# Fold parts of a Fourier mixing kernel issued one step earlier, and the first batch's folds and mixes at other steps

## The chip, the cores and the metric

The kernel runs on one core of a Trainium2 chip. The metric is device time in microseconds (us). The engines are named as the profile names them: PE (TensorE matmuls), PEld (its weight loads), DVE (VectorE), ACT (ScalarE), POOL (GpSimd) and SP (SyncE, which here only issues DMAs). The kernel's data is float32 throughout.

## The reference

The input x has 8 batches of 3008 rows by 256 columns. Each batch is Fourier transformed along its rows and along its columns, and the real part is kept. The result, seen as 24064 rows, goes through a layer with 2048 hidden units.

```python
X = np.fft.fft(x, axis=1)
X = np.fft.fft(X, axis=2)
y = X.real.astype(np.float32).reshape(B * S, D)      # (24064, 256)
h = y @ w_in                                         # w_in (256, 2048)
g = h * (1.0 / (1.0 + np.exp(-1.702 * h)))
out = g @ w_out                                      # w_out (2048, 256)
```

## The kernel before

**Two kinds of work share the engines.** The transform of a batch comes first: its x is loaded into one large tile `xt` (`load_x`, L205), folded on POOL (`fold1`: sums and differences of mirrored columns and rows, in place), multiplied by cosines and sines on PE (`mix1`, L255), copied back into `xt` by ACT (`mixed`, L263), spilled to memory (`spill`, L339) and read back in another layout (`fill`, L345). A second stage on PE (`stage2`, L365) makes the operands `pq` of the hidden layer. The column transform is folded into `w_in`, which gives the weights `wcs`. While PE, ACT and DVE work through the hidden layer of batch b, the transform of batch b+1 is slipped in between.

**Steps.** The hidden layer runs in 384 steps t, 48 for each batch: 3 blocks, 2 halves of a block, and 8 steps p = t mod 8, each with two of the 16 groups of 128 hidden units. The first 8 steps of the program have a form of their own (`hidden`, `rows`). From t = 8 a step works as follows, each engine in this program order:

- PE makes the pre-activations: `begin(t, 1)` and `begin(t+1, 0)` (L184, into `x`). Bank `x` is filled beforehand by ACT with a rank-one term, two steps ahead: `middle(t+2)` (L585).
- ACT applies the activation to one half (`forward`, L600), doubles the sum (`doubled`, L597) and applies it to the other half (`activate_back`, L607), which DVE has made (`backward`, L604).
- The product with `w_out` uses a fast matrix multiplication of Strassen's kind, so that sums and differences of activations are needed: `sums(t, nc.gpsimd)` on POOL (L615, L616), `sums(t-1, nc.vector)` on DVE every second step (L622, L623), and a second level on DVE, `deeper` (L646 and L648 in odd steps, L650 in even ones).
- PE multiplies three steps later: `product(t-3)` (L184, into `o`) and `small_products` (L684, into `low` and `o`). At the first step after an output sum, the small products 5, 6 and 3 of the old group come right after `begin(t, 1)` (the flag `opening`, L1040).

**Output sums.** Every 8 steps an output is complete. It is put together in the steps p = 2 (`combine`, L754 to L758), 3 (`combine_small`, L786), 4 (`swap` L794 to L796 on ACT, `combine_last` L768 and L804) and 5 and 6 (`turn_last`, the transpose L737 on DVE, then stores on SP).

**Work of the transform.** A table `extra` lists calls to be made at the end of a step: `at(t, fn, ...)`. The folds of one batch are 16 calls: 8 chunks c, each with part 0 (L225, L227; for chunk 0 also three operations into the tile `e`, L218 to L220) and part 1 (L230, L231). Four calls, those of two chunks, make a group, and `mix1` of that group follows. POOL runs in order, so a fold part issued at the end of step t stands behind the sums of t and before the sums of t+1.

**What a mix changes in its step.** A step whose list holds `mix1` or `stage2` is called special (L1028). The mix takes the bank that x(t) has left, so `middle(t+2)` is not issued in that step but at the start of the next, and PE's order in the next step is another one (`after`, L1028: the products come ahead of `begin`).

**The table.** `PLANS` (L932) holds two plans, the first for b = 0 and the second for all later ones. Each has the 16 steps of the fold parts, the 4 steps of the groups, and the step of the first of three fills, counted from the first step of batch b. For later batches the folds of group m lay at 8m - 1, 8m, 8m + 1 and 8m + 2, which is p = 7, 0, 1, 2, and its mix at 8m + 7. Spills follow one step after a mix. `load_x` of batch b+2 is issued at steps 36, 38, 40 and 42 of batch b, `rotate` at 39, and `stage2` at 8, 24 and 40. In the first batch's steps 5 to 10 the last weights are made as well: differences on POOL (`differences`, L482) and on DVE (`small_weights`, L695).

Of the kernel before, what the change touches and what calls it, by code (L numbers as in the profile page):

```python
# [112 lines left out]
def kernel(ctx: ExitStack, tc, x, w_in, w_out, tab1, tab2, out):  # L113
# [815 lines left out]
    finish_out(0)  # L929

    extra, early = {}, {}
    PLANS = ((range(11, 27), (16, 20, 25, 28), 32), ([g + k for g in (0, 8, 16, 24) for k in range(-1, 3)], (7, 15, 23, 31), 33))  # L932

    def at(t, fn, *args):
        extra.setdefault(t, []).append((fn, args))
# [23 lines left out]
    for b in range(B):  # L959
# [5 lines left out]
        if b + 1 < B:  # L965
            folds, groups, filled = PLANS[min(b, 1)]
            for c in range(NCH):
                for part in range(2):
                    at(t0 + folds[2 * c + part], fold1, b + 1, c, part, nc.gpsimd)
                if c % 2:  # L970
                    k = t0 + groups[c // 2]
# [140 lines left out]
```

## Time and profile before

| | us |
|---|---|
| median of 3 runs | 1852.71 (1851.91 to 1855.34) |
| the profiled execution | 1851.27 |
| its span, first to last instruction | 1849.5 |
| PE busy | 1835.5 |
| DVE busy | 1485.5 |
| ACT busy | 1148.6 |
| POOL busy | 1001.1 |

Views used: the page; the list of waits (engine and line, what it waited for, us in total, times, longest); stretches (from:to, us, then busy us and count of PE, PEld, DVE, ACT and POOL, granted clock, share of the DMA queues' time, GB/s); and rows in order of time (start us, duration us, engine, line, operation, out<-in, count, and in brackets the idle time before it with what ended it). A row of the timeline may hold several equal instructions. A duration in the timeline counts from when the engine took the instruction up, so it contains any time in which the instruction was held up.

### The profile page before, as it was taken

The numbers are of one execution on the slowest core, as the hardware profiler recorded it, in microseconds if no ns is written. First come the engines' busy times: TensorE is split into PE (matmuls) and PEld (weight loads), VectorE is DVE, ScalarE is ACT, GpSimd is POOL, SyncE is SP. The second block draws the span as 40 slices with busy tenths as digits, with TensorE's granted clock in tenths as the row PEclk, the third lists the DMA queues.
The fourth block names the chain that finished last, engine by engine and source line by source line (L and its number), as shares of the span: only waits on it lengthen the run. The fifth ranks groups of instructions, "written<-read, shape, count | busy, mean of one in ns | idle before, by whom it ended". The sixth has DMA issues, their size and how long they took to land.

```text
span 1849.5 us, 55986 instructions
## 1 busy us (share of the span) xinstructions
PE 1835.5 (99%) x23722; PEld 1411.0 (76%) x23722; DVE 1485.5 (80%) x1928; ACT 1148.6 (62%) x2241; POOL 1001.1 (54%) x1053
## 2 busy tenths in 40 slices
PE   8999999999999999999999999999999999999998
PEld 5677777777777777777777777777788777778776
DVE  6988778887888778877788778878888788878875
ACT  5666656666666666666665666666655666656663
POOL 4786456554556546565365544656446654444442
PEclk9999999999999999999999999999999999999999
DMA  8721341214211151211502115121241112100111
GB/s 285 178 61 34 87 65 28 55 32 103 44 48 40 33 112 29 60 33 48 109 13 71 33 48 97 22 72 26 71 73 23 35 26 56 30 19 13 23 19 24
DMA packets 149706, 105.31 MB, mean 57 GB/s; under 512 B 106057, under 2 KB 130665, under 8 KB 148896
## 3 DMA queue, kind: packets, MB, share of 16 engines
q1 hardware_dynamic: 146624, 99.68, 24.0%
q8 instruction: 187, 3.06, 0.7%
q10 hardware_dynamic: 2832, 2.05, 0.5%
q14 instruction: 63, 0.52, 0.1%
HBM read 64.41 MB, written 48.05 MB: 61 GB/s over the span
## 4 chain that ended last, share of the span: by engine, by line
PE 88%; DVE 8%; DMA 2%; ACT 1%; issue 1%; POOL 0%; SPq 0%; DVEq 0%; ACTq 0%; POOLq 0%
PE x L184 32%; PE o L184 25%; PE low L684 23%; PE o L684 4%; PE ps L255 2%; DVE big L650 2%; PE ps L365 1%; DVE big L622 1%; DVE big L604 1%; DVE big L786 1%; DVE big L648 1%; DVE big L646 1%; DMA xt<-in_x_dram 1%; DMA Td<-big 1%; DVE big L804 0%
## 5 line engine op out<-in xcount | busy, mean ns | idle before, releaser
L615 POOL TENSOR_TENSOR big<-big 128x256 f32<-128x256 f32 (+1 forms) x376 | 357.9, 952 | 797.0 <-ACT big L607 694.5
L184 PE MATMUL x<-pq,wcs 128*64 128x256 f32 (+1 forms) x6016 | 776.8, 376 | 1.0 <-ACT x L585 0.4
L184 PE MATMUL o<-big,wo 128*64 128x256 f32 (+1 forms) x4800 | 629.0, 375 | 0.6 <-issue 0.6
L184 PEld LDWEIGHTS x<-pq,wcs 128*64 128x64 f32 x6016 | 421.9, 137 | 175.9 <-issue 15.3
L184 PEld LDWEIGHTS o<-big,wo 128*64 128x64 f32 x4800 | 348.0, 137 | 145.9 <-issue 1.0
L597 ACT ACTIVATE g<-x 128x512 f32<-128x512 f32 (+1 forms) x376 | 221.8, 590 | 379.9 <-PE x L184 378.6
L604 DVE TENSOR_TENSOR big<-g,x 128x512 f32<-128x512 f32 (+1 forms) x376 | 250.8, 667 | 186.5 <-ACT big L600 186.4
L616 POOL TENSOR_TENSOR big<-big 128x256 f32<-128x256 f32 (+1 forms) x376 | 399.6, 1063 | 0.0
L585 ACT ACTIVATE x<-nb,af 128x256 f32<-128x256 f32 (+1 forms) x752 | 353.0, 469 | 69.1 <-DVE pq L372 55.9
L684 PE MATMUL low<-big 128*64 128x128 f32 (+1 forms) x5888 | 386.1, 270 | 0.0
L684 PEld LDWEIGHTS low<-big 128*64 128x64 f32 x5888 | 341.0, 137 | 27.9
L600 ACT ACTIVATE big<-x 128x512 f32<-128x512 f32 (+1 forms) x376 | 219.2, 583 | 123.5 <-PE x L184 113.6
L646 DVE TENSOR_TENSOR big<-big 128x1024 f32<-128x1024 f32 (+1 forms) x184 | 234.1, 1272 | 65.2 <-PE low L684 41.4
L607 ACT ACTIVATE big<-big 128x512 f32<-128x512 f32 (+1 forms) x376 | 231.7, 616 | 37.2 <-DVE big L604 35.4
L684 PE MATMUL low<-big,wo 128*64 128x128 f32 (+1 forms) x2944 | 224.8, 271 | 1.4 <-DVE big L650 0.7
L648 DVE TENSOR_TENSOR big<-big 128x512 f32<-128x512 f32 (+1 forms) x184 | 177.1, 963 | 15.9
L650 DVE TENSOR_TENSOR big<-big 128x512 f32<-128x512 f32 (+1 forms) x184 | 185.4, 1007 | 0.0
L684 PEld LDWEIGHTS low<-big,wo 128*64 128x64 f32 x2944 | 175.4, 137 | 6.4 <-DVE big L650 2.9
L622 DVE TENSOR_TENSOR big<-big 128x512 f32<-128x512 f32 (+1 forms) x188 | 140.7, 748 | 3.3 <-POOL big L615 3.3
L623 DVE TENSOR_TENSOR big<-big 128x512 f32<-128x512 f32 (+1 forms) x188 | 135.6, 721 | 6.5
L684 PEld LDWEIGHTS o<-big,wo 128*64 128x64 f32 x1472 | 94.3, 137 | 24.3
L684 PE MATMUL o<-big,wo 128*64 128x128 f32 (+1 forms) x1472 | 112.2, 270 | 0.0
(97 smaller groups left out, 1144.6 us busy)
## 6 DMA issues: line engine op xcount, KB each, us to landing
out_dram<-os SPq DMA_DIRECT2D x284, 64.0 KB
t<-Td SPq DMA_DIRECT2D x22, 512.0 KB
Td<-xt SPq DMA_DIRECT2D x56, 192.0 KB
xt<-in_x_dram SPq DMA_DIRECT2D x14, 512.0 KB
xt<-Xr SPq DMA_DIRECT2D x14, 512.0 KB
nb<-Nd SPq DMA_DIRECT2D x23, 256.0 KB
out_dram<-os SPq DMA_DIRECT2D x96, 56.0 KB
Xr<-in_x_dram SPq DMA_DIRECT2D x7, 752.0 KB
```

The lines of the kernel that those rows point to most:

```text
L184: nc.tensor.matmul(out[c0:c0 + 64], lhsT=lhs[:, c0:c0 + 64], rhs=rhs, skip_group_check=True, **how)
L585: nc.scalar.activation(x[:, i * 256:i * 256 + n], nbt[b, blk][:, hh * 256:hh * 256 + n], ACTF.Copy, scale=af1[:, f:f + 1])
L597: nc.scalar.activation(two(g[:], n), two(xb[t][:], n), ACTF.Copy, scale=2.0)
L600: nc.scalar.activation(front(t), two(xb[t][:], width(t)), ACTF.Gelu_apprx_sigmoid)
L604: nc.vector.tensor_tensor(back(t), two(gt.pop(t)[:], n), two(xb.pop(t)[:], n), op=ALU.subtract)
L607: nc.scalar.activation(back(t), back(t), ACTF.Gelu_apprx_sigmoid)
L615: eng.tensor_tensor(right(t, S1, n), left(t, A21, n), right(t, A22, n), op=ALU.add)
L616: eng.tensor_tensor(left(t, S3, n), left(t, A11, n), left(t, A21, n), op=ALU.subtract)
L646: nc.vector.tensor_tensor(free(big[:], SUM, *both_), free(big[:], from11 + w, *twice), free(big[:], from11, [at_right(t, 0) + w - from11, ...
L648: nc.vector.tensor_tensor(s2, a11, s1, op=ALU.subtract)
L650: nc.vector.tensor_tensor(s4, a12, s2, op=ALU.subtract)
L684: nc.tensor.matmul(o, lhsT=lhs, rhs=rhs, start=first_in, stop=(p == NP - 2), skip_group_check=True)
```

## The change

Only the table changes. In the second plan the four fold parts of a group lie at p = 6, 7, 0, 1. In the first plan the folds lie at steps 9 to 17, 22 to 26, 29 and 30, the groups at 15, 17, 26 and 31, and the three fills begin at 33 instead of 32. Spills move with their mixes. Nothing is added or left out: every operation is issued once as before, on the same engine.

```diff
-    PLANS = ((range(11, 27), (16, 20, 25, 28), 32), ([g + k for g in (0, 8, 16, 24) for k in range(-1, 3)], (7, 15, 23, 31), 33))
+    PLANS = (((*range(9, 18), 22, 23, 24, 25, 26, 29, 30), (15, 17, 26, 31), 33),
+             ([g + k for g in (0, 8, 16, 24) for k in range(-2, 2)], (7, 15, 23, 31), 33))
```

The table is read by these lines, which are unchanged:

```python
folds, groups, filled = PLANS[min(b, 1)]
for c in range(NCH):
    for part in range(2):
        at(t0 + folds[2 * c + part], fold1, b + 1, c, part, nc.gpsimd)
    if c % 2:
        k = t0 + groups[c // 2]
        at(k, mix1, b + 1, c // 2)
        for half in range(2):
            at(k + 1, spill, b + 1, half, c // 2)
```

## The prediction

> **What bounds the kernel now.** I read the page first: busy shares, then the chain that ended last.
>
> ```profile
> PE 1835.5 (99%) x23722; PEld 1411.0 (76%) x23722; DVE 1485.5 (80%) x1928; ACT 1148.6 (62%) x2241; POOL 1001.1 (54%) x1053
> PE 88%; DVE 8%; DMA 2%; ACT 1%; issue 1%; POOL 0%; SPq 0%; DVEq 0%; ACTq 0%; POOLq 0%
> ```
>
> TensorE is full, and what the edit moves runs on POOL, which is not on the chain at all. So the change can only be worth something where POOL slows DVE and DVE slows PE. The modelled ends of matmuls hide short stalls, so I next asked who the weight loads (PEld) waited for, in batches 1 to 6 (260 to 1580 us) and in batch 0 (80 to 260 us).
>
> ```profile
> PEld x L184 <- ACT x L585: 4.4, 12, 0.8
> PEld low L684 <- DVE big L650: 2.0, 6, 0.3
> ```
>
> ```profile
> PEld low L684 <- DVE big L650: 0.9, 1, 0.9
> PEld o L184 <- DVE big L622: 0.5, 1, 0.5
> ```
>
> The first two lines are batches 1 to 6, the others batch 0. Six waits for L650 mean one in each batch. To find the steps I cut the time at the first x matmul of each step: 48 steps a batch, p = t mod 8. Apart from t = 14 and t = 19 of the batch (and the steps that hold a mix1 or a stage2) equal steps last equally long nearly everywhere. Step 14 (batches 1, 2, 7) and step 19 (batches 1, 7) are, in the view by stretches:
>
> ```profile
> 334.33:338.90 4.57, 4.44 (x63) 3.47 (x61) 4.43 (x7) 3.42 (x8) 2.25 (x3) 1.00 0.13 25
> 558.43:563.23 4.80, 4.44 (x63) 3.47 (x60) 4.66 (x8) 3.41 (x8) 2.25 (x3) 1.00 0.11 20
> 1678.78:1683.07 4.29, 4.29 (x62) 3.46 (x60) 4.15 (x7) 3.41 (x8) 2.24 (x3) 1.00 0.14 27
> 356.87:361.39 4.52, 4.40 (x57) 3.18 (x54) 4.35 (x7) 2.48 (x7) 3.96 (x6) 1.00 0.00 0
> 1699.87:1704.05 4.18, 4.18 (x56) 3.18 (x54) 3.23 (x7) 2.48 (x7) 1.53 (x3) 1.00 0.01 4
> ```
>
> Batch 7 has no folds, since no batch follows it. With folds step 14 costs 0.28 us more (0.51 in batch 2; batches 3 to 6 are like batch 1) and step 19 costs 0.34 more. That is all that folds cost in the steady batches: 5 x 0.28 + 0.51 = 1.91 and 6 x 0.34 = 2.04 us.
>
> **The steady batches, step 19.** A fold part issued at the end of step t runs on POOL in step t+1, behind the sums. Part 0 (L225, L227) was issued at odd t, part 1 (L230, L231) at even t; now it is the other way round.
>
> ```profile
> 579.36 0.68 DVE L622 TENSOR_TENSOR big<-big 128x512 f32<-128x512 f32 x1
> 580.19 1.70 POOL L227 TENSOR_TENSOR xt<-xt 111x510 f32<-111x510 f32 x1
> 581.85 0.73 POOL L615 TENSOR_TENSOR big<-big 128x256 f32<-128x256 f32 x1
> 580.68 2.38 DVE L650 TENSOR_TENSOR big<-big 128x452 f32<-128x452 f32 x1
> 583.12 0.39 PEld L684 LDWEIGHTS low<-big,wo 128*64 128x64 f32 x8 [0.33 <-DVE big L650]
> 1699.36 0.62 DVE L650 TENSOR_TENSOR big<-big 128x452 f32<-128x452 f32 x1
> ```
>
> L650 takes 0.62 us alone and 2.38 beside L227 and L615: it gets nothing until both are through, and the first small products after an output sum wait for it. After the change the slot at t = 17 holds part 1, and t = 18 holds nothing. How a DVE operation fares beside part 1 shows in batch 0:
>
> ```profile
> 115.95 0.72 POOL L230 TENSOR_TENSOR xt<-xt 111x254 f32<-111x254 f32 x1
> 116.02 1.66 DVE L646 TENSOR_TENSOR big<-big 128x904 f32<-128x904 f32 x1 [0.65 <-ACT big L607]
> 116.63 1.63 POOL L231 TENSOR_TENSOR xt<-xt 111x254 f32<-111x254 f32 x1
> ```
>
> L646 waits for L230 alone and then goes ahead of L231, which takes 1.63 instead of 0.72: they alternate. In step 18 L622 would hold POOL's L230 off until 580.04, then L230 (0.72), L623 (0.68 like L622), L231 (0.72) and L650 (0.62) follow: L650 ends at 582.8 instead of 583.06, against a need at 583.12 - 0.33 = 582.8. I take the stall as gone: -2.04. Bounds: nothing gained, or 0.6 us added per batch if L231 and L615 both go ahead of L650.
>
> The Trainium skill, SBUF — State Buffer, "Who interferes with whom", has a shared port pair held for a whole instruction, and whoever issues first goes first. The trace agrees with the blocking, but not with the order: L650 had begun to wait at 580.68 and L615, from 581.85, still went before it. By the rule the old stall would not exist and the steady sum would lack these 2.04 us.
>
> **Step 14.** The chain starts four steps earlier, in the output sum of steps 10 to 13 (batch 2, then batch 7 without folds):
>
> ```profile
> 543.85 1.27 POOL L227 TENSOR_TENSOR xt<-xt 111x510 f32<-111x510 f32 x1
> 544.07 1.53 DVE L622 TENSOR_TENSOR big<-big 128x452 f32<-128x452 f32 x1
> 545.63 1.12 DVE L623 TENSOR_TENSOR big<-big 128x452 f32<-128x452 f32 x1
> 1664.42 0.62 DVE L622 TENSOR_TENSOR big<-big 128x452 f32<-128x452 f32 x1
> 1667.02 0.42 DVE L757 TENSOR_TENSOR big<-big,o 128x256 f32<-128x256 f32 x1 [0.72 <-ACT big L754]
> 560.49 0.58 PEld L184 LDWEIGHTS x<-pq,wcs 128*64 128x64 f32 x8 [0.76 <-ACT x L585]
> ```
>
> With folds L622 and L623 take 2.65 us, where batch 7 needs 0.62 for the first and as much for the second; L650 behind them is stretched as well. DVE then has no pause until step 13, so its L604, and ACT's L607 and L585 behind that, come late, and x(15) waits. After the change L230 and L231 stand in L227's place, and the part that followed at t = 10 is gone. The three operations then wait for two parts of 0.72 less what already overlaps, some 1.2 us. Batch 7 has slack for most of it right behind them: L757 waits 0.72 for ACT, and L604 of step 11 waits again. So step 14 falls to batch 7's 4.29: -1.91. Bounds: 0 and -1.91.
>
> **Other steady slots.** Part 0 now runs in odd steps, where DVE is nearly free at first (3.16 us of step 33), and the fold at p = 6 before a new batch needs x loaded:
>
> ```profile
> 200.34:203.50 3.16, 3.16 (x40) 2.29 (x38) 0.69 (x1) 0.98 (x3) 0.90 (x2) 1.00 0.28 97
> L218 POOL TENSOR_TENSOR e<-xt x1: 715/715/715, 271.7 to 271.7; 47x254 f32<-47x254 f32 x1
> 251.00:263.00 12.00, 12.00 (x142) 9.03 (x140) 11.69 (x15) 9.29 (x18) 6.59 (x6) 1.00 0.01 3
> ```
>
> DVE works 0.69 us there, so part 0 finds the port free. From 251 the queues carry 1%, so the loads are in. The fold moves from 271.7 to about 267: 16 us are left, and the move costs nothing. Were that cover gone, POOL would hold its sums behind the load. The SP queue keeps its order in these batches, since mixes, spills and fills stay where they are; in batch 0 its spills and fills move, with 5 steps or more before rotate at 39 reads what they bring.
>
> **Batch 0.** Its folds lie at 9 to 17, 22 to 26, 29 and 30 now, and its mixes at 15, 17, 26 and 31 instead of 16, 20, 25 and 28. No fold runs in steps 19 to 22, so the waits of 0.9 (step 19, L650) and 0.5 (step 23, L622) above should go. I take 0.9 and 0.4, and 0.1 for step 15, where the later e part is out of the way: -1.4. A mix at p = 4 (steps 20 to 22), one at p = 7 (31 to 33 of batch 2) and the same steps without:
>
> ```profile
> 135.46:150.61 15.15, 15.15 (x190) 11.30 (x188) 14.84 (x16) 11.47 (x23) 12.41 (x13) 1.00 0.04 8
> 195.58:209.44 13.86, 13.86 (x174) 10.82 (x172) 9.28 (x13) 8.08 (x17) 6.30 (x7) 1.00 0.32 99
> 638.51:653.11 14.60, 14.60 (x184) 10.83 (x182) 8.76 (x11) 8.35 (x17) 5.25 (x7) 1.00 0.27 58
> 191.24:204.68 13.44, 13.44 (x169) 10.40 (x167) 7.62 (x10) 7.29 (x15) 4.99 (x7) 1.00 0.33 86
> ```
>
> 1.29 against 1.16: 0.13 for each mix moved to an odd step, about -0.4 for three. The mix at 26 stands between an output sum and the next use of its banks: it puts that use off by its own 1.1 us while ACT and DVE drain them as before, so I take no new wait. The mix at 17 follows its last fold part by one step instead of two. Batch 2 has a mix and folds in the same places up to there:
>
> ```profile
> 575.11 0.72 POOL L231 TENSOR_TENSOR xt<-xt 111x254 f32<-111x254 f32 x1
> ```
>
> L231 of t = 16 ends at 575.8. PE ends step 17 a whole step 18 (4.42 us, the same in every batch) ahead of 581.20, at 576.8, so 1 us is left and I take 0; without it PE would stand for what is missing, at most some 0.7.
>
> Against this stands step 12. The first part, with its three copies into e, moves from t = 11 to t = 9, and so beside the last small_weights (L695):
>
> ```profile
> 91.53 0.67 POOL L616 TENSOR_TENSOR big<-big 128x226 f32<-128x226 f32 x1
> 97.31 0.38 DVE L695 TENSOR_TENSOR big<-wo 128x256 f32<-128x256 f32 x1
> 82.54 0.95 DVE L695 TENSOR_TENSOR big<-wo,big 128x256 f32<-128x256 f32 x1
> 99.39 0.58 ACT L607 ACTIVATE big<-big 128x452 f32<-128x452 f32 x1 [0.58 <-DVE big L604]
> 100.85 0.58 PEld L184 LDWEIGHTS x<-pq,wcs 128*64 128x64 f32 x8 [0.44 <-ACT x L585]
> ```
>
> POOL was idle here. Now from 92.2 it runs the e part (three operations near L218's 0.7) and L225 and L227 (1.3), some 4 us with waits, then sums and part 1 of t = 10, each about 0.7, until about 100.6. So three of the four L695 wait one POOL operation each: 3 x 0.7 = 2.1. A contended L695 takes 0.95 instead of 0.4, so 4 x 0.55 = 2.2 says the same. L604 behind them is already what L607, L585 and x(13) wait for, so the whole comes out at PE: +2.0. Bounds: 0, if POOL is through earlier, and 2.8, four waits. Later steps start as much later and find POOL 2 us less behind. Batch 0 sums to -1.4 - 0.4 + 2.0 = +0.2.
>
> **Sum.** -2.04 - 1.91 + 0.2 = -3.8 us. The profiled execution took 1851.27 us (span 1849.5 and 1.77 around it), so it would take 1847.5; the median of the runs is 1.44 higher, 1852.71, which gives 1848.9.
>
> **The rivals.** One: L695 does not collide, and batch 0 keeps its 1.8: -3.95 - 1.8 = -5.7, 1847.0. For it: POOL's times here are only worked out; against it: the 0.95 that L695 took beside POOL's differences. Two: at step 19 L231 and L615 both go ahead of L650, as L615 did at 581.85. The stall is then 0.6 instead of 0.34: -1.91 + 1.6 + 0.2 = -0.1, 1852.6. Against it: the alternation at 116. The page's rule gives this no chance, the row at 581.85 gives it some. Three: the wait in step 14 and that in step 19 are the output sum's own and the folds hide behind it anyway: 1852.9. Batch 7 speaks against it. Four, slower: POOL keeps the port through a whole run of its operations.
>
> ```profile
> 149.20 2.91 DVE L622 TENSOR_TENSOR big<-big 128x512 f32<-128x512 f32 x1
> ```
>
> This L622 lost to L227, L615 and L616 in turn. If L230, L231, L615 and L616 (4 x 0.72) all went ahead in step 18, L623 and L650 would end at 580.04 + 2.88 + 1.31 = 584.2, a stall of 1.4 instead of 0.34 in six batches: +6.4 - 1.91 + 0.2 = +4.7, 1857.4. It decides once L650 ends past about 583.5. Against it: L231 let DVE through at 117.
>
> **How the numbers follow.** Forecast 0.56, rival one 0.15, two 0.12, three 0.07, four 0.10. Two tenths of a per cent, 3.7 us, is what a measurement can tell from no change, and the forecast of -3.8 lies right at it. I give 0.38 of its 0.56 to faster, since the unresolved small waits (L585 in six more places) lean that way, and 0.18 to no change. Faster: 0.38 + 0.15 = 0.53. Same: 0.18 + 0.12 + 0.07 = 0.37. Slower: 0.10. The likeliest case alone spans 1847.5 to 1850.5; with rivals one to three and a microsecond for the runs the range is 1845.8 to 1853.6.
>
> **What would show it.** Steps 14 at 4.3 and 19 at 4.18 in batches 1 to 6, and the list of waits of PEld without L650 there; L650 in step 18 ending within 1.2 us of step 19's start. In batch 0, a wait of about 2.4 us for L585 near 101, L695 at 0.7 to 1.1, and no waits for L650 or L622. The forecast is wrong if step 19 keeps its wait, if a wait appears in odd steps behind L646 or L648, or if mix1 at t = 17 waits for L231 of t = 16.

## The result and the profile after

| | before | after |
|---|---|---|
| median of 11 runs each, us | 1851.91 (1850.80 to 1855.34) | 1847.79 (1846.69 to 1848.66) |
| ratio of the times, 95% interval | | 0.9975 [0.9967, 0.9982] |
| the profiled execution, us | 1851.27 | 1848.23 |
| its span, us | 1849.5 | 1846.4 |

The kernel is 4.1 us faster in the medians; the forecast was 3.8. The ratio lies 0.25% below 1, just past the 0.2% that the prediction called measurable, and its interval (0.18% to 0.33%) wholly below 1.

From the page of the changed kernel, the busy shares and the chain that ended last:

```profile
PE 1832.7 (99%) x23722; PEld 1403.0 (76%) x23722; DVE 1487.9 (81%) x1928; ACT 1148.3 (62%) x2241; POOL 1007.7 (55%) x1053
...
PE 97%; DMA 2%; DVE 0%; ACT 0%; SPq 0%; issue 0%; POOL 0%; DVEq 0%; ACTq 0%; POOLq 0%
```

DVE has gone from 8% of the chain to nothing. DVE and POOL are busy a little longer than before, 2.4 and 6.6 us: they hold each other up more, in places where nothing waits for them (one of them is shown under rival four below). A busy sum that grows while the kernel gets faster is no contradiction here, because a duration counts from when the engine took the instruction up.

The waits of the weight loads in batches 1 to 6 (260 to 1577 us):

```profile
PEld ps L365 <- DVE big L650: 2.2, 13, 0.2
PEld x L184 <- ACT x L585: 1.3, 5, 0.3
...
PEld x L184 <- ACT g L597: 0.3, 1, 0.3
```

The row for `low` behind L650 (2.0 us, six times) is gone, and L585 fell from 4.4 to 1.3. What is left of L650 stands at the stage2 steps and was there before. By stretches, step 14 and step 19 of batch 1, then all of batch 0, of batches 1 to 6, and steps 12 and 27 of batch 0:

```profile
336.22:340.50 4.28, 4.28 (x62) 3.46 (x60) 4.14 (x7) 3.40 (x8) 2.24 (x3) 1.00 0.14 25
358.48:362.66 4.18, 4.18 (x56) 3.17 (x54) 4.01 (x7) 2.48 (x7) 2.46 (x4) 1.00 0.00 0
81.92:271.73 189.81, 188.09 (x2457) 143.01 (x2454) 152.11 (x198) 115.56 (x228) 115.70 (x128) 1.00 0.29 61
271.73:1612.83 1341.10, 1341.06 (x17726) 1040.60 (x17724) 1097.83 (x1411) 844.73 (x1669) 750.53 (x789) 1.00 0.24 51
100.99:106.39 5.40, 4.44 (x62) 3.46 (x60) 4.68 (x8) 3.29 (x7) 3.46 (x4) 1.00 0.59 116
172.73:178.04 5.31, 4.55 (x56) 3.23 (x53) 3.61 (x8) 3.18 (x7) 1.89 (x3) 1.00 0.26 72
```

The same stretches of the kernel before, without steps 14 and 19, which the prediction shows:

```profile
80.15:269.84 189.69, 188.90 (x2457) 143.17 (x2455) 155.22 (x198) 115.77 (x228) 115.48 (x124) 1.00 0.29 61
269.84:1615.88 1346.04, 1343.80 (x17726) 1048.55 (x17724) 1092.66 (x1411) 844.80 (x1669) 742.44 (x793) 1.00 0.23 50
99.12:103.59 4.47, 4.44 (x62) 3.46 (x60) 3.75 (x6) 3.30 (x7) 3.54 (x3) 1.00 0.53 120
171.76:176.09 4.33, 4.33 (x56) 3.33 (x54) 2.95 (x7) 3.01 (x8) 2.79 (x4) 1.00 0.38 106
```

The two profiles differ by 3.1 us, in four parts:

- What comes ahead of step 8 takes 81.92 us instead of 80.15, +1.8. In the twelve profiles of this case, each of another kernel, it lies between 80.15 and 84.98 us. The plans start only at step 9, so it isn't counted as theirs.
- Batch 0: +0.1.
- Batches 1 to 6: -4.9. Step 14 fell in all six, together by 1.97 us, and step 19 by 2.03. Steps 12 and 13 of batch 5 are 0.26 longer; this is the wait for L597 above, and the run of the first plan alone, whose second plan is that of before, has it too. The remaining 1.2 us are no steady gain: 0.8 is at step 42 of batch 5, most of the rest at steps 3 and 7 of batch 6.
- Batch 7, without folds: 227.8 from its first step to the last matmul in both.

The 0.8 us at step 42 is a wait that the kernel before has in the row "PEld o L184 <- issue: 1.0, 1, 1.0" of its list of waits. All ten experiments below have it too, whatever their plans, and only this profile lacks it. It isn't counted as a gain.

How the gain in step 19 comes about shows in step 18 of batch 2 (577.55 to 581.97), from the timeline of the changed kernel:

```profile
580.13 0.68 DVE L622 TENSOR_TENSOR big<-big 128x512 f32<-128x512 f32 x1
580.16 1.23 POOL L230 TENSOR_TENSOR xt<-xt 111x254 f32<-111x254 f32 x1
...
580.85 1.10 DVE L623 TENSOR_TENSOR big<-big 128x512 f32<-128x512 f32 x1
...
581.35 1.17 POOL L231 TENSOR_TENSOR xt<-xt 111x254 f32<-111x254 f32 x1
581.87 1.15 DVE L650 TENSOR_TENSOR big<-big 128x452 f32<-128x452 f32 x1
...
582.49 1.12 POOL L615 TENSOR_TENSOR big<-big 128x256 f32<-128x256 f32 x1
```

Put in order of their ends, they are L622, L230, L623, L231, L650, L615: one operation of DVE, one of POOL, in turn. All but the first are stretched, by 0.4 to 0.5 us, and none loses two turns. L650 takes 1.15 us instead of 2.38 and ends 1.05 us after the start of step 19.

The hold alone costs nothing; what counts is when PE needs the result. In the kernel before, L650 took 2.45 us behind L227 and L615 in step 2 of each of these batches as well, and in batches 1 to 5 step 3 lasted no longer than in batch 7 (4.33). There L650 ended 1.43 us into step 3; in batch 6 it was 1.74, and step 3 took 0.11 more. In step 18 it ended 1.86 us into step 19, and PE could have used it 1.59 us into it.

For step 14, two rows of batch 2 (step 10 begins at 543.05):

```profile
545.34 0.70 DVE L622 TENSOR_TENSOR big<-big 128x452 f32<-128x452 f32 x1
...
561.25 0.58 PEld L184 LDWEIGHTS x<-pq,wcs 128*64 128x64 f32 x8 [0.25 <-ACT x L585]
```

L622 takes 0.70 us instead of 1.53, and L650 ends 5.15 us into step 10 instead of 6.04. DVE then has 0.25 us of idle time ahead of L604 of step 11, where it had none, and x(15) waits 0.25 us for L585 instead of 0.76.

Batch 0 kept its length, but not its steps. The waits of the weight loads there (80 to 260 us):

```profile
PEld x L184 <- ACT x L585: 2.0, 3, 1.4
...
PEld x L184 <- ACT g L597: 1.2, 1, 1.2
```

No wait for L650 or L622 is left, as forecast. A wait of 1.4 for L585 stands in step 12 (+0.93 us), and one of 1.2 for L597 in step 27 (+0.98), which the prediction did not have. Against these stand -0.90 in step 19, -0.40 in step 23, and -0.6 in the mixes' steps and step 15; step 9 gives +0.1. In step 12 the delay is on DVE, beside part 1 on POOL (step 12 begins at 100.99):

```profile
99.08 0.71 POOL L230 TENSOR_TENSOR xt<-xt 111x254 f32<-111x254 f32 x1
99.18 0.90 DVE L695 TENSOR_TENSOR big<-wo 128x256 f32<-128x256 f32 x1
...
100.12 0.83 DVE L695 TENSOR_TENSOR big<-wo,big 128x256 f32<-128x256 f32 x1
...
100.87 0.41 DVE L695 TENSOR_TENSOR big<-wo 128x256 f32<-128x256 f32 x1
...
103.65 0.58 PEld L184 LDWEIGHTS x<-pq,wcs 128*64 128x64 f32 x8 [1.36 <-ACT x L585]
```

Two of the four L695 meet a part of the fold (0.90 and 0.83 instead of 0.41), and their 0.91 us go through L604, L607 and L585 to PE. Step 27 is of another kind. From its timeline, the rows around its end at 178.04:

```profile
177.39 0.60 ACT L597 ACTIVATE g<-x 128x512 f32<-128x512 f32 x1 [1.90 <-PE x L184]
...
178.04 0.20 PEld L184 LDWEIGHTS x<-pq,wcs 128*64 128x64 f32 x4 [1.21 <-ACT g L597]
```

PE ends `begin(28, 0)`, ACT doubles it, and `begin(28, 1)` can only start then. In other steps products or small products stand between the two. Step 27 is `opening` and follows a mix: the code brings its products and the old group's small products ahead of `begin(28, 0)`, and the trace shows no matmul between that and `begin(28, 1)`.

### The profile page after: what moved, and what is told of

It reads as the page before. It is cut to its first block, busy times and chain, and to the rows that moved or that the text cites. A ratio compares the mean times of both kernels' runs of the same rounds, so it can differ in the third digit from the quotient of the medians.

```text
span 1846.4 us, 55977 instructions
## 1 busy us (share of the span) xinstructions
PE 1832.7 (99%) x23722; PEld 1403.0 (76%) x23722; DVE 1487.9 (81%) x1928; ACT 1148.3 (62%) x2241; POOL 1007.7 (55%) x1053
## 4 chain that ended last, share of the span: by engine, by line
PE 97%; DMA 2%; DVE 0%; ACT 0%; SPq 0%; issue 0%; POOL 0%; DVEq 0%; ACTq 0%; POOLq 0%
PE x L184 35%; PE o L184 27%; PE low L684 26%; PE o L684 4%; PE ps L255 2%; PE ps L365 1%; DMA big<-in_moe_w_in_dram 1%; DMA xt<-in_x_dram 1%; PE po L184 0%; PE psw L184 0%; DMA big<-in_moe_w_out_dram 0%; PE pb L184 0%; PE pa L184 0%; PE low L184 0%; DVE big L695 0%; DMA Td<-e 0%
## 5 line engine op out<-in xcount | busy, mean ns | idle before, releaser
L615 POOL TENSOR_TENSOR big<-big 128x256 f32<-128x256 f32 (+1 forms) x376 | 362.2, 963 | 784.2 <-ACT big L607 651.9
L184 PE MATMUL x<-pq,wcs 128*64 128x256 f32 (+1 forms) x6016 | 768.5, 376 | 1.8 <-ACT x L585 1.0
L184 PE MATMUL o<-big,wo 128*64 128x256 f32 (+1 forms) x4800 | 620.9, 375 | 0.0
L184 PEld LDWEIGHTS x<-pq,wcs 128*64 128x64 f32 x6016 | 415.0, 137 | 180.0 <-issue 15.3
L597 ACT ACTIVATE g<-x 128x512 f32<-128x512 f32 (+1 forms) x376 | 221.8, 590 | 381.0 <-PE x L184 379.8
L184 PEld LDWEIGHTS o<-big,wo 128*64 128x64 f32 x4800 | 341.6, 137 | 146.4
L616 POOL TENSOR_TENSOR big<-big 128x256 f32<-128x256 f32 (+1 forms) x376 | 408.5, 1086 | 0.0
L604 DVE TENSOR_TENSOR big<-g,x 128x512 f32<-128x512 f32 (+1 forms) x376 | 250.8, 667 | 181.2 <-ACT big L600 181.1
L585 ACT ACTIVATE x<-nb,af 128x256 f32<-128x256 f32 (+1 forms) x752 | 352.9, 469 | 68.6 <-DVE pq L372 55.5
L684 PE MATMUL low<-big 128*64 128x128 f32 (+1 forms) x5888 | 381.4, 270 | 0.0
L646 DVE TENSOR_TENSOR big<-big 128x1024 f32<-128x1024 f32 (+1 forms) x184 | 253.6, 1378 | 66.3 <-PE low L684 41.8
L607 ACT ACTIVATE big<-big 128x512 f32<-128x512 f32 (+1 forms) x376 | 231.6, 616 | 37.3 <-DVE big L604 35.7
L684 PE MATMUL low<-big,wo 128*64 128x128 f32 (+1 forms) x2944 | 220.1, 270 | 0.0
L648 DVE TENSOR_TENSOR big<-big 128x512 f32<-128x512 f32 (+1 forms) x184 | 181.7, 988 | 15.9
L650 DVE TENSOR_TENSOR big<-big 128x512 f32<-128x512 f32 (+1 forms) x184 | 170.2, 925 | 0.0
L623 DVE TENSOR_TENSOR big<-big 128x512 f32<-128x512 f32 (+1 forms) x188 | 137.9, 734 | 6.5
L622 DVE TENSOR_TENSOR big<-big 128x512 f32<-128x512 f32 (+1 forms) x188 | 129.7, 690 | 1.7 <-POOL big L615 1.7
L786 DVE TENSOR_TENSOR big<-big,low 128x512 f32<-128x512 f32 (+3 forms) x184 | 109.1, 610 | 3.8
L684 PEld LDWEIGHTS o<-big,wo 128*64 128x64 f32 x1472 | 92.3, 137 | 24.9
```

What stands on the lines that cost most here:

```text
L184: nc.tensor.matmul(out[c0:c0 + 64], lhsT=lhs[:, c0:c0 + 64], rhs=rhs, skip_group_check=True, **how)
L585: nc.scalar.activation(x[:, i * 256:i * 256 + n], nbt[b, blk][:, hh * 256:hh * 256 + n], ACTF.Copy, scale=af1[:, f:f + 1])
L597: nc.scalar.activation(two(g[:], n), two(xb[t][:], n), ACTF.Copy, scale=2.0)
L604: nc.vector.tensor_tensor(back(t), two(gt.pop(t)[:], n), two(xb.pop(t)[:], n), op=ALU.subtract)
L607: nc.scalar.activation(back(t), back(t), ACTF.Gelu_apprx_sigmoid)
L615: eng.tensor_tensor(right(t, S1, n), left(t, A21, n), right(t, A22, n), op=ALU.add)
```

## The experiments

**The two plans apart.** First the second plan alone, then the first plan alone.

```diff
-    PLANS = ((range(11, 27), (16, 20, 25, 28), 32), ([g + k for g in (0, 8, 16, 24) for k in range(-1, 3)], (7, 15, 23, 31), 33))
+    PLANS = ((range(11, 27), (16, 20, 25, 28), 32),
+             ([g + k for g in (0, 8, 16, 24) for k in range(-2, 2)], (7, 15, 23, 31), 33))
```

> Only the second plan is changed (folds at p = 6, 7, 0, 1), the first plan is that of before. Theory (POOL's L227 no longer stands beside L622 in step 10 and L650 in step 18): in batches 1 to 6 step 14 is 4.29 and step 19 is 4.18, the batches take 223.5 us, and the time is 3.9 us (0.21%) under before; batch 0 keeps its wait for L650 at step 19 (5.08) and for L622 at step 23. Rival (part of the gain comes from the first batch): under 3 us is gained here.

Measured: 1848.58 us against 1852.42 before in the same series, ratio 0.9974 [0.9962, 0.9985]. Batch 0, batches 1 to 6, and steps 14 and 19 of batch 1:

```profile
82.23:271.90 189.67, 188.87 (x2457) 143.13 (x2455) 155.18 (x198) 115.79 (x228) 117.98 (x128) 1.00 0.28 61
271.90:1613.77 1341.87, 1341.52 (x17727) 1052.78 (x17724) 1098.28 (x1411) 845.24 (x1669) 749.52 (x789) 1.00 0.24 51
336.39:340.67 4.28, 4.28 (x63) 3.47 (x61) 4.14 (x7) 3.41 (x8) 2.25 (x3) 1.00 0.14 26
358.64:362.82 4.18, 4.18 (x56) 3.18 (x54) 4.01 (x7) 2.48 (x6) 2.47 (x4) 1.00 0.00 0
```

```diff
-    PLANS = ((range(11, 27), (16, 20, 25, 28), 32), ([g + k for g in (0, 8, 16, 24) for k in range(-1, 3)], (7, 15, 23, 31), 33))
+    PLANS = (((*range(9, 18), 22, 23, 24, 25, 26, 29, 30), (15, 17, 26, 31), 33),
+             ([g + k for g in (0, 8, 16, 24) for k in range(-1, 3)], (7, 15, 23, 31), 33))
```

> Only the first plan is changed, the second is that of before. Theory: batch 0 loses its waits at 19 and 23 (1.3 us) and pays 0.9 at step 12 and 1.0 at step 27, so it takes 189.8 as before and the time is that of before within 0.5 us; batches 1 to 6 keep 4.57 (4.80) at step 14 and 4.52 at step 19. Rival (the first plan carries part of the gain): 1 us or more is gained.

Measured: 1852.31 us, ratio 0.9999 [0.9990, 1.0007]. Batch 0:

```profile
82.55:272.26 189.71, 188.00 (x2456) 143.04 (x2454) 151.99 (x198) 115.54 (x228) 113.07 (x124) 1.00 0.29 61
```

The whole gain comes from the second plan. The first plan is worth nothing (189.71 us where the kernel before has 189.69), with the same pattern of steps inside it as in the changed kernel: 5.40 at step 12, 5.31 at 27, 4.18 at 19, 4.33 at 23. So batch 0 didn't stay the same because nothing happened there; gains and new waits of about 1.9 us each cancel.

**Which fold part, in which step.** Three other second plans: the parts at p = 0 to 3, the last part alone moved to p = 3, and the parts at p = 5, 6, 7, 0. The first is built on the changed kernel, the other two on the kernel before.

```diff
-             ([g + k for g in (0, 8, 16, 24) for k in range(-2, 2)], (7, 15, 23, 31), 33))
+             ([g + k for g in (0, 8, 16, 24) for k in range(0, 4)], (7, 15, 23, 31), 33))
```

> The changed kernel with the second plan's folds at p = 0, 1, 2, 3: inside the output sum, with part 0 at even t as after the change. Theory (what counts at step 19 is which part runs beside L650 in step 18): L650 takes about 1.15 us there and step 19 stays at 4.18 in batches 1 to 6; in step 12, where part 1 of t = 11 now runs beside L622 and L623, DVE loses 1 to 1.5 us in the chain to L604 of step 13, so step 14 waits again, 4.6 to 5.2. Rival (a fold at p = 2 is the harm, whichever part): step 19 is 4.5 or more too.

Measured in a single run: 1855.49 us (before on the same chip: 1851.38). Steps 19 and 14 of batch 1:

```profile
358.69:362.87 4.18, 4.18 (x56) 3.17 (x54) 4.01 (x7) 2.48 (x7) 3.91 (x6) 1.00 0.00 0
335.82:340.71 4.89, 4.44 (x62) 3.47 (x60) 4.75 (x8) 3.41 (x8) 2.24 (x3) 1.00 0.12 23
```

```diff
-    PLANS = ((range(11, 27), (16, 20, 25, 28), 32), ([g + k for g in (0, 8, 16, 24) for k in range(-1, 3)], (7, 15, 23, 31), 33))
+    PLANS = ((range(11, 27), (16, 20, 25, 28), 32),
+             ([g + k for g in (0, 8, 16, 24) for k in (-1, 0, 1, 3)], (7, 15, 23, 31), 33))
```

> The kernel before with only the fold part at p = 2 moved to p = 3 in the second plan (p = 7, 0, 1, 3). Theory (L227, issued at p = 1, is what holds L650 and L622): step 19 keeps 4.52 with L650 at about 2.4, step 14 keeps 4.5 or more. Rival (the part at p = 2, inside the output sum, is what costs): step 19 falls to 4.18 and step 14 to about 4.3.

Measured in a single run: 1863.35 us (its step 8 began at 83.74 us, 3.6 later than in the kernel before). Step 14 of batch 1 took 5.17 us; step 19:

```profile
361.38:365.90 4.52, 4.39 (x56) 3.17 (x54) 4.35 (x7) 2.48 (x7) 2.60 (x4) 1.00 0.00 0
```

These two settle step 19. In the first, t = 17 issues part 1 and t = 18 still issues a part (POOL does six operations in step 19, the changed kernel four), and the wait is gone. In the second, t = 17 issues part 0 as before and t = 18 nothing, and the wait of 0.34 us is there to the hundredth. So it is L227 in step 18 that costs, not the part that followed in step 19. Both also show what a fold late in an output sum costs: besides step 14, steps 6, 22 and 30 of batch 1, each 4.77 us long in both kernels, grew to between 4.83 and 5.11. In batches 1 to 6 the waits for L585 grew to 12.5 and 16.0 us, from 4.4.

```diff
-    PLANS = ((range(11, 27), (16, 20, 25, 28), 32), ([g + k for g in (0, 8, 16, 24) for k in range(-1, 3)], (7, 15, 23, 31), 33))
+    PLANS = ((range(11, 27), (16, 20, 25, 28), 32),
+             ([g + k for g in (0, 8, 16, 24) for k in range(-3, 1)], (7, 15, 23, 31), 33))
```

> The kernel before with the second plan's folds at p = 5, 6, 7, 0: part 0 at odd t as before the change, but nothing at p = 1 and 2. Theory (L227 must stand in step 18 to hold L650, in step 10 to hold L622; parity only matters through that): step 19 is 4.18 and step 14 is 4.29 to 4.4, batches 1 to 6 take 223.5, as after the change. Rival (part 0 in even steps costs wherever it runs beside DVE's work): waits of 0.2 us or more turn up at step 14 or 16, and batches take 223.8 or more.

Measured in a single run: 1853.12 us. Steps 14 and 19 gained as in the changed kernel (4.29 and 4.18), but step 15, which neither the theory nor the rival had named, went from 5.06 to 5.92 in batches 1 to 6 and took it all back. From its timeline, batch 1, whose step 15 begins at 339.58:

```profile
338.14 1.27 POOL L227 TENSOR_TENSOR xt<-xt 111x510 f32<-111x510 f32 x1
...
338.43 2.72 DVE L622 TENSOR_TENSOR big<-big 128x452 f32<-128x452 f32 x1
...
339.37 0.67 POOL L615 TENSOR_TENSOR big<-big 128x226 f32<-128x226 f32 x1
...
340.00 0.67 POOL L616 TENSOR_TENSOR big<-big 128x226 f32<-128x226 f32 x1
...
341.20 0.20 PEld L184 LDWEIGHTS o<-big,wo 128*64 128x64 f32 x4 [0.70 <-DVE big L622]
...
343.84 0.58 DVE L604 TENSOR_TENSOR big<-g,x 128x452 f32<-128x452 f32 x1
...
344.47 0.64 PEld L255 LDWEIGHTS ps<-xt,w 47*64 47x64 f32 x16 [0.55 <-DVE big L604]
```

This is the run of POOL operations that the slower rival was made of: L622 waits through L227, L615 and L616 and takes 2.72 us. It is paid for twice, once by the product that needs L622's result, and once by the mix, which takes over the bank that L604 reads and so waits for a DVE that is late. One step earlier than p = 6, 7, 0, 1 loses what the move gained; one step later is the plan of before.

**The two waits of batch 0.** Three kernels built on the changed one: the third mix at 25 instead of 26, so that no mix precedes step 27; the last four L695 at the end of t = 14 instead of t = 10; and both.

```diff
-    PLANS = (((*range(9, 18), 22, 23, 24, 25, 26, 29, 30), (15, 17, 26, 31), 33),
+    PLANS = (((*range(9, 18), 22, 23, 24, 25, 26, 29, 30), (15, 17, 25, 31), 33),
```

> The changed kernel with the third mix of the first plan at 25 instead of 26, nothing else. Theory (step 27 waits because the mix in step 26 makes PE put begin(28) last in a step that opens an output, with nothing of its own to do until ACT's L597 has read it): step 27 falls from 5.31 to 4.33, no PEld wait for L597 there, step 12 stays at 5.40; batch 0 takes about 188.9. Rival (an output sum right before step 27 is late by itself): step 27 keeps about 1 us of wait.

Measured in a single run: 1851.0 us, in an execution whose step 8 began at 84.62 us, 2.7 us later than in the changed kernel's profile. Batch 0 took 189.25 us; in it steps 27 and 31:

```profile
175.33:179.67 4.34, 4.34 (x57) 3.33 (x55) 2.96 (x7) 3.02 (x9) 2.78 (x4) 1.00 0.38 98
193.53:199.56 6.03, 5.85 (x73) 3.59 (x69) 6.00 (x6) 2.02 (x4) 3.54 (x5) 1.00 0.24 42
```

Step 27 fell from 5.31 to 4.34, as the explanation above has it. But step 31, which holds the last mix, went from 5.46 to 6.03, which was not expected. Its timeline:

```profile
191.83 1.27 POOL L227 TENSOR_TENSOR xt<-xt 111x510 f32<-111x510 f32 x1
192.11 2.91 DVE L622 TENSOR_TENSOR big<-big 128x512 f32<-128x512 f32 x1
...
193.06 0.74 POOL L615 TENSOR_TENSOR big<-big 128x256 f32<-128x256 f32 x1
...
193.74 0.74 POOL L616 TENSOR_TENSOR big<-big 128x256 f32<-128x256 f32 x1
...
198.53 0.64 PEld L255 LDWEIGHTS ps<-xt,w 47*64 47x64 f32 x16 [0.56 <-DVE big L604]
```

It is the same sequence as with the parts at p = 5: part 0 at t = 29 lies at p = 5. In the changed kernel L622 of that step is taken up 2.40 us into the step and gets through behind L227 in 1.53; here it is 3.34 us into it, and POOL's next sums are there at once. That the stall at step 27 had given DVE this time is what the two traces suggest.

```diff
-        at(7 + i, small_weights, i)
+        at(14 if i == 3 else 7 + i, small_weights, i)
```

> The changed kernel with the last small_weights call at t = 14 instead of 10, nothing else. Theory (L604 of step 11 stands behind four L695, two of which wait for L230 and L231): L604 starts about 1.9 us sooner, step 12 falls from 5.40 to 4.2 to 4.5, step 27 stays at 5.31, and step 15 takes the four L695 without a new wait. Rival (POOL's own sums are late): step 12 stays at 5.4.

Measured in a single run: 1848.81 us (before: 1851.38). Step 12 of batch 0 took 4.21 us; step 15:

```profile
113.05:119.67 6.62, 5.57 (x78) 4.12 (x74) 5.94 (x7) 1.97 (x4) 5.11 (x6) 1.00 0.01 2
```

Step 12 lost all of its wait, and step 15 grew from 5.48 to 6.62. The four L695, stretched to 0.8 to 0.9 us each by POOL, stand ahead of L604 of step 15, and the mix at the end of that step waits 1.5 us for it (in the list of waits "PEld ps L255 <- DVE big L604: 1.5, 1, 1.5"). The wait was moved, not removed.

> The changed kernel with the third mix of the first plan at 25 instead of 26 and the last small_weights call at t = 14 instead of 10. Theory (step 12's wait is L604 behind L695 beside POOL's L230 and L231; step 27's wait is begin(28) as the last work of a step that is both opening and after a mix): step 12 is 4.2 to 4.5 instead of 5.40, step 27 is 4.33 instead of 5.31, batch 0 takes 188.0 instead of 189.8 and the time is 1.5 to 2.0 us under the changed kernel's, 5.5 to 6.0 under before (ratio 0.9970). Rival for step 12 (the chain is late for POOL's sake, not DVE's): step 12 keeps 5.4. Rival for step 27 (the output banks are drained late): step 27 keeps a wait whatever the mix before it.

Measured: 1848.40 us, ratio 0.9970 [0.9959, 0.9982]; batch 0 took 189.32 us, 1.3 more than expected. It is the sum of the two: steps 12 and 27 at 4.22 and 4.33, steps 15 and 31 at 6.63 and 6.02.

**Where the waits have room.** In the changed kernel DVE has nothing to do for 2.0 us ahead of L604 of step 10. So, on the changed kernel, the last four L695 at t = 9; and, on top of that, the third mix at 25 and the last fold parts at 30 and 31, p = 6 and 7, with the last mix at 32 and the fills from 34.

```diff
-        at(7 + i, small_weights, i)
+        at(min(7 + i, 9), small_weights, i)
```

> The changed kernel with the last four L695 at the end of t = 9, behind the four that stand there already, instead of t = 10. In the changed kernel's trace DVE is idle from the last L695 of that place to L604 of step 10, 2.0 us, and four L695 take 1.6 us alone. Theory: step 12 goes from 5.40 to 4.22 and no later step pays for it, so batch 0 goes from 189.80 to about 188.6 us and the kernel to about 1846.6. Rival: as in the two kernels that moved them to t = 14, the wait only moves: L604 of step 10 comes late beside POOL's L615 and L616, and step 10 or 11 grows by 0.5 us or more (batch 0 at 189.2 or more).

Measured: 1846.59 us against 1851.71, ratio 0.9974 [0.9964, 0.9985]. Step 12 took 4.21 us; batch 0:

```profile
81.45:270.07 188.62, 187.86 (x2457) 143.14 (x2455) 151.48 (x198) 115.55 (x228) 116.18 (x128) 1.00 0.29 62
```

```diff
-    PLANS = (((*range(9, 18), 22, 23, 24, 25, 26, 29, 30), (15, 17, 26, 31), 33),
+    PLANS = (((*range(9, 18), 22, 23, 24, 25, 26, 30, 31), (15, 17, 25, 32), 34),
```

> As the run with the last four L695 at t = 9, and besides the third mix at t = 25 instead of 26, the last two fold parts at t = 30 and 31 instead of 29 and 30, the last mix at 32 instead of 31 and the fills from 34. Theory: the wait of 0.57 us that came up in step 31 once the mix stood at 25 came from part 0 at p = 5, whose L227, followed by L615 and L616, kept L622 for 2.9 us and made L604 of step 31 late for the mix; with part 0 at p = 6 that is gone. Then step 27 lasts 4.33, step 31 no more than 4.5, and the mix one step later costs 0.13 more for standing in an even step: batch 0 at about 187.8 us and the kernel at about 1845.8. Rival: the mix in step 32 waits for L231 of the same step or for a late L604: batch 0 at 188.3 or more.

Measured: 1847.16 us (1845.28 to 1850.14), ratio 0.9975 [0.9966, 0.9984]. Steps 27 and 31 took 4.33 us each. Batch 0:

```profile
84.98:272.50 187.52, 187.52 (x2457) 143.25 (x2454) 150.37 (x198) 115.59 (x228) 115.13 (x128) 1.00 0.28 61
```

Both did in batch 0 what was expected: 188.62 and 187.52 us, 1.2 and 2.3 less than the changed kernel, with no new wait behind. In the second one PE is busy for the whole of batch 0. The medians cannot carry this: against the changed kernel's 1847.79 the two are 1.2 and 0.6 us lower, their intervals overlap the changed kernel's, and the start of the loop alone varies by more (the profile of the second one has it at 84.98 us). Both beat the kernel before; that they also beat the changed one is shown in batch 0 of the profiles, not in the total.

## Why the prediction came out as it did

**Step 19 (-2.04 forecast, -2.03 measured).** Right in size and in mechanism: L622, L230, L623, L231 and L650 take turns, as the prediction laid them out. It put L650's end 1.58 us into step 19, with a slack of nothing; it came at 1.05, because the four turns behind L622 took 0.50 to 0.58 us each and not 0.62 to 0.72. In every plan run here, step 19 of batches 1 to 6 waits where L227 stands in step 18, and in no other. Rival two, L231 and L615 both ahead of L650, did not happen: L615 came after L650. (The bound of 0.6 us added per batch doesn't fit that rival's own working: a stall of 0.6 instead of 0.34 adds 0.26.)

**Step 14 (-1.91 forecast, -1.97 measured).** Right: the step is at batch 7's 4.29 or below in all six batches, by the chain that the prediction laid out. Where the parts of steps 10 to 13 come late (p = 0 to 3) it is 4.89. That batch 7's values came back in both steps refutes rival three, that the waits are the output sum's own. Two limits remain. No run has L227 in step 10 without another part behind it in step 11 or 12, so the price of L227 alone is open. And some 0.24 of both numbers, the excess of batch 2 (4.80 instead of 4.57), is not the folds' price: the run of the first plan alone keeps the second plan of before and has 4.56 there. In batch 2 of the kernel before, POOL's L615 was taken up 0.03 us ahead of L650 of step 13 and went first; in the other batches, and in that run, L650 went first although it came up to 0.02 us after L615.

**Batch 0 (+0.2 forecast, +0.1 measured).** Right in the sum by luck: two errors cancel, one in step 12 and one in step 27. The waits of 0.9 and 0.4 us went as forecast. The mixes and step 15 came to -0.6 (-0.5 forecast), but not term by term. The prediction took 0.13 for each of three mixes moved to odd steps and left out that the third goes the other way, from 25 to 26, which at its own price would cost 0.13. By steps, the first mix with step 15 gave -0.10, the second -0.36, the third with step 24 -0.09 and the fourth -0.05. The term that was mis-sized is step 12: +2.0 forecast, +0.93 measured. The step that failed is the estimate that POOL works until about 100.6, which had three of the L695 waiting. The prediction's own terms, some 4 us from 92.2 and then four operations of 0.7, end at 99.0; 1.6 us of the 100.6 had no row behind it. In the trace POOL was through at 100.66, 0.3 us before step 12, where the prediction had it 1.5 us after the start of that step. Only two L695 met it, and lost 0.49 and 0.42 us where the prediction took 0.7 for each.

**What the prediction lacked.** "The mix at 26 [...] I take no new wait" is the step that failed: it looked for who waits for the banks that the mix puts off, and found nobody. It didn't look at how a mix changes PE's order in the step after it. Step 27 is also `opening`, and the two together leave nothing between `begin(28, 0)` and `begin(28, 1)`; +0.98. Taking the mix to 25 removes it, so `opening` alone doesn't make the wait. Neither does a mix alone: the other three mixes of batch 0 are followed by steps that are not `opening`, and the list has only one wait of 1.2 for L597.

**The sum.** -2.03 - 1.97 + 0.1 is -3.9 us, against -3.8 forecast and 4.1 between the medians.

**The mix at 17 and the moved loads (nothing forecast).** The list of waits of the changed kernel has no row for a mix behind POOL's folds, in batch 0 or later. L231 of t = 16 ended 1.05 us before the mix at 17 began, where the prediction had 1 us left. Batches 1 to 6 have no new wait apart from the one of 0.3 us for L597, which isn't the second plan's.

**Rival four, POOL through a whole run of operations.** It does not occur in step 18, where the prediction put it, but the changed kernel has it elsewhere. In step 47 of batches 0 to 5 part 0 of the first chunk, which has the operations into `e` ahead of it, meets L646; in batch 1:

```profile
494.13 3.65 DVE L646 TENSOR_TENSOR big<-big 128x1024 f32<-128x1024 f32 x1 [0.79 <-PE low L684]
```

L646 gets through only after L227 (from 494.05), L615 and L616. It takes 1.21 us where nothing holds it up. So "part 0 finds the port free", which the prediction read from step 33, is wrong for this slot; no weight load waits for L646 there, so it costs nothing. In two timelines of the experiments, with part 0 at p = 5, the same run of three holds L622 for 2.72 and 2.91 us, and there PE waits.

The Trainium skill, SBUF — State Buffer, "Who interferes with whom", has whoever issues first go first on the shared port pair. The trace agrees for step 18, where the six operations went in the order in which they were taken up, from 580.13 to 582.49. It differs in step 30 of the kernel with its mix at 25: there L622 had been waiting since 192.11, and L615 and L616, from 193.06 and 193.74, both went before it. The measurement decides.

## What to carry to other kernels

Where two engines hold each other up, the cost of a helper's operation depends on which operation it meets and on what is queued right behind it: place it by the steps in which the other engine has idle time ahead of it, and read that from the trace of a stretch without the helper, as batch 7 was here. A wait that is moved comes back unless its new place has idle time on the engine that pays, as the same four operations showed at two places, and a stall that is removed can uncover the next one, as step 31 suggests, where the stall at step 27 seems to have given DVE time to catch up. A total that comes out right doesn't vouch for its terms; only a cut into steps showed that two of them were wrong by a microsecond each.

## What was not expected of the hardware

- DVE and POOL mostly take turns, but POOL sometimes goes through three operations in a row while DVE waits: L622 at 2.72 us (0.62 alone) and at 2.91 (0.68 alone), and L646 at 3.65 (1.21 alone). In all three, L227 had taken 1.27 us, without a wait of its own, and L615 and L616 followed at once. In step 30 of the changed kernel L227 took 1.27 as well, but L615 came 0.67 us after its end, and L622 went in between. What decides is not settled: behind an L227 that had waited itself, L615 went ahead of L650 in the kernel before (L227 at 1.70 us), while in step 14 of batch 0 of the changed kernel L650 got in first (L227 at 1.65, L650 at 1.71, L615 at 1.05 instead of 0.66).
- What comes ahead of step 8 took between 80.15 and 84.98 us in the profiles of these kernels. Its cause is open; it is larger than the effect of the change.
- A single wait of 0.7 to 1.1 us in step 42 of batch 5 appears in eleven of the twelve profiles; the changed kernel's is the one without. The profile names no engine for it, only "issue".
